# A table of places in a list scheduler's order: every operation named by class, 45 classes moved, three of the scheduler's figures changed

## The chip, the cores and the metric

The kernel runs on one core of a Trainium2 chip. The metric is device time in microseconds. The core has five engines with queues of their own: PE (TensorE, matrix products, with its weight loads shown as PEld), DVE (VectorE), ACT (ScalarE), POOL (GpSimd) and SP (SyncE, which here only issues DMAs). An engine works through its own instructions in the order in which the program gave them and waits at semaphores for the others.

## The reference

Three layers on 2304 tokens of width 512, in fp32:

```python
# attention with random features (4 batches, 8 heads, 576 tokens, head width 64, 128 features)
h = x @ omega.T - sum(x*x)/2;  phi = exp(h - max(h)) / sqrt(128)      # for q and k, both scaled
kv = k_p^T v;  z = sum(k_p);   out = (q_p kv) / (q_p z + 1e-6)
# eight experts, all of them for every token, gates P normalized by 8 Sinkhorn rounds
P = exp(x @ w_gate - max); repeat 8: P /= rowsum; P /= colsum; P *= N/E
out += P[:, e] * (relu(x @ w1[e]) @ w2[e])                            # w1[e] 512x1024, w2[e] 1024x512
# one MLP
g = h * sigmoid(1.702 h),  h = x @ w_in;  out = g @ w_out              # 512x2048 and 2048x512
```

## The kernel before

**Products.** Tokens lie in three blocks of 768 (the "columns" of the program's outer loop, j = 0, 1, 2). The hidden width is worked through in 20 "pairs" of 2 x 256: 16 pairs for the eight experts, two for each, then 4 for the MLP. For each pair and block (a "visit") the products up and down are done with a Strassen scheme of seven products of half-size blocks in place of eight. Each operand is split into a high and a low part that TensorE's fast fp32 form can take, and each product is three matmuls with the terms high-high, high-low and low-high. `up_fast` issues the up products (L1210, 128x384), `down_across` those of the experts' down step (L1364, 128x384), `down` those of the MLP (L1401, 128x256).

**What surrounds them.** After each up product ACT copies banks of PSUM to other banks, to the `ring` in SBUF, or into `h`, the high part of an operand (all L1220, in `act` and `operand`). DVE adds and subtracts banks (L1231), multiplies by the gate (L1252) and makes low parts; low parts from the ring and the sums in the ring are made on POOL or DVE by the helper `tt` (L440). The weights of the next pair are loaded by DMA into `raw`, summed there (L440 on `raw`), and split: ACT makes the high part (L1116, in `split`), POOL the low part (L440 on `w1x`, `w2x`), in three pieces for each of two columns c, one of 128x768 and two of 128x512. After the experts the blocks of x for the MLP are built in the same way by `y_operands` (tiles `acc`, `x2s`; in this stretch POOL does most of it). `double_piece` turns the MLP's weights, which arrive in double precision, into fp32 by six bit steps on DVE (L1140 to L1156) and one sum on POOL, between 440 and 1400 us.

**Attention** runs first, to about 143 us: transposes on PE, copies on ACT, the features' max (L628) and the division (L737, L742, L745) on DVE, exponentials on ACT (L650), squares on POOL. `x_parts` then transposes its results (L785) and splits them (ACT L803, DVE L806) into the operands of the first pairs.

**What sets the order.** The program doesn't issue its instructions as it is written. Each is recorded as an `Op` in a `Plan` with an engine, an estimated duration, and the keys it reads and writes; `VP` means DVE or POOL, `AV` means ACT or DVE. PE's main operations keep their written order. `deadlines` gives each other operation a time `late` at which it must begin so that the main operations that hang on it are not held up: it goes back from each successor's `late` and takes off `LAT` and the operation's duration. `run` then plays all engines through in time. An engine that is free takes, among the operations whose inputs are there, the one with the smallest `late`:

```python
late = min((s.late for s in o.succ), default=total + 50.0) - self.LAT - self.least(o)
...
if e == "DVE" and slack > self.BELOW and len(both) < 14:
    flex = None                       # DVE leaves a VP operation with that much time to POOL
...
at[e] = o.end if e in ("PE", "X") else o.end - self.LEAP
```

`LAT` is the time from an engine to another, `LEAP` how far an engine's next instruction overlaps the last. What `run` returns is the order in which the instructions are written to the engines' queues; the chip's semaphores, not the planned times, decide when they run.

## Time and profile before

| what | us |
|---|---|
| median of 3 runs (1954.36, 1960.79, 1962.69) | 1960.79 |
| the profiled execution's own time | 1957.73 |
| its span in the trace | 1955.8 |
| PE busy | 1925.2 |
| DVE, POOL, ACT busy | 1392.0, 1374.2, 1051.7 |

The profile is of one execution. Busy is the time in which an engine had an instruction at work; it says nothing of whether others waited. Matmuls follow each other closer than one lasts, so TensorE can lose time without a gap in its busy time. The timeline merges like instructions that follow each other into one row with a count. Releasers ("<-") are inferred from semaphores.

### The profile page before, as it was taken

Reading aid. Unit: us, or ns where it says so; the run is one execution under the profiler, and the core shown is the slowest. Engines: PE = TensorE matmul, PEld = TensorE weight load, DVE = VectorE, ACT = ScalarE, POOL = GpSimd, SP = SyncE. Lnnn points to the kernel's source line nnn. Section 1 sums busy time; section 2 is a strip of 40 time slices with the busy share of each in tenths; the row PEclk is TensorE's granted clock in tenths of the full one; section 3 lists DMA queues with packets and bytes.
Section 4 is the critical chain, followed back from the end, with each engine's and each line's share of the span. In section 5 each row is a group of like instructions: output and inputs, shape, how many; then the busy total and the mean of one; then the engine's idle time right before and its main releaser. Section 6 shows DMA issues by size and latency. Waiting matters only on the chain. (4 is left out here: it accounts for less than half of the span.)

```text
span 1955.8 us, 36203 instructions
## 1 busy us (share of the span) xinstructions
PE 1925.2 (98%) x12899; PEld 1883.9 (96%) x12899; DVE 1392.0 (71%) x2704; ACT 1051.7 (54%) x2400; POOL 1374.2 (70%) x1387
## 2 busy tenths in 40 slices
PE   8999999999999999999999999999999989999999
PEld 7888999999999999999999999999999989999999
DVE  6874467767778778778778778778666684656655
ACT  7985554444535445445536345454446476755654
POOL 7965475987759596777769596867758895837452
PEclk9999999999999999999999999999999999999999
DMA  9777556667668576667667576677666788745653
GB/s 175 192 203 245 190 194 244 228 217 279 227 237 293 210 270 257 237 257 267 231 253 272 213 287 243 236 273 254 221 233 252 272 300 316 258 182 201 240 207 125
DMA packets 259292, 464.04 MB, mean 237 GB/s; under 512 B 75288, under 2 KB 200104, under 8 KB 259112
## 3 DMA queue, kind: packets, MB, share of 16 engines
q1 hardware_dynamic: 259112, 461.74, 67.5%
q8 instruction: 101, 1.65, 0.3%
q14 instruction: 79, 0.65, 0.1%
HBM read 415.45 MB, written 46.21 MB: 236 GB/s over the span
## 5 line engine op out<-in xcount | busy, mean ns | idle before, releaser
L1210 PE MATMUL bank<-xo,w1x 128*128 128x384 f32 x5040 | 916.6, 336 | 5.1 <-ACT bank L1220 1.9
L1210 PEld LDWEIGHTS bank<-xo,w1x 128*128 128x128 f32 x5040 | 874.7, 188 | 12.5 <-ACT bank L1220 6.1
L1364 PE MATMUL bank<-h,w2x 128*128 128x384 f32 x4032 | 728.8, 337 | 2.3 <-DVE h L1231 1.3
L1364 PEld LDWEIGHTS bank<-h,w2x 128*128 128x128 f32 x4032 | 700.7, 188 | 8.0 <-POOL h L440 3.4
L440 POOL TENSOR_TENSOR h<-ring,h 128x384 fp32r<-128x384 f32 x452 | 458.2, 1043 | 77.7 <-ACT h L1220 69.3
L1382 DVE TENSOR_TENSOR acc<-bank,acc 128x384 f32<-128x384 f32 x552 | 294.1, 557 | 218.0 <-PE bank L1364 211.0
L440 POOL TENSOR_TENSOR w1x<-raw,w1x 128x768 fp32r<-128x768 f32 (+1 forms) x120 | 179.4, 1504 | 213.1 <-ACT w1x L1116 213.0
L1220 ACT ACTIVATE ring<-bank 128x384 f32<-128x384 f32 x480 | 234.9, 493 | 151.1 <-PE bank L1210 141.6
L1220 ACT ACTIVATE bank<-bank 128x384 f32<-128x384 f32 x216 | 103.6, 482 | 387.7 <-PE bank L1210 358.7
L440 POOL TENSOR_TENSOR raw<-raw 128x256 f32<-128x256 f32 x311 | 242.2, 804 | 75.5 <-DMA raw<-in_moe_w_dram 60.9
L1220 ACT ACTIVATE h<-ring 128x384 fp32r<-128x384 f32 x480 | 237.8, 530 | 77.1 <-DVE ring L1231 71.2
L1231 DVE TENSOR_TENSOR h<-bank,h 128x384 fp32r<-128x384 f32 x324 | 179.0, 553 | 113.4 <-ACT ring L1220 88.9
L440 POOL TENSOR_TENSOR ring<-ring 128x384 f32<-128x384 f32 x114 | 121.2, 1063 | 160.1 <-ACT ring L1220 111.1
L1231 DVE TENSOR_TENSOR ring<-bank,ring 128x384 f32<-128x384 f32 x432 | 223.7, 550 | 9.4 <-ACT bank L1220 6.2
L1252 DVE SCALAR_TENSOR_TENSOR bank<-bank,x2s 128x384 f32<-128x384 f32 x336 | 185.1, 558 | 57.5 <-PE bank L1210 56.8
L1220 ACT ACTIVATE h<-bank 128x384 fp32r<-128x384 f32 x360 | 177.2, 493 | 42.5 <-DVE bank L1252 27.2
L440 POOL TENSOR_TENSOR w2x<-raw,w2x 128x768 fp32r<-128x768 f32 (+1 forms) x120 | 183.9, 1545 | 16.2 <-ACT w2x L1116 15.5
L1401 PE MATMUL bank<-w2x,h 128*128 128x256 f32 x1512 | 186.8, 281 | 5.1 <-POOL w2x L440 2.4
L1401 PEld LDWEIGHTS bank<-w2x,h 128*128 128x128 f32 x1512 | 183.3, 189 | 7.5 <-POOL w2x L440 2.6
L1116 ACT CAST w2x<-raw 128x512 fp32r<-128x512 f32 (+1 forms) x120 | 80.2, 692 | 130.9 <-POOL raw L440 121.6
L1231 DVE TENSOR_TENSOR bank<-bank,ring 128x384 f32<-128x384 f32 x240 | 134.1, 559 | 16.3 <-PE bank L1210 14.6
L1427 DVE TENSOR_TENSOR acc<-bank,acc 128x256 f32<-128x256 f32 x180 | 68.0, 419 | 47.0 <-PE bank L1401 40.9
(134 smaller groups left out, 1263.7 us busy)
## 6 DMA issues: line engine op xcount, KB each, us to landing
xo<-sx SPq DMA_DIRECT2D x413, 768.0 KB, 7.0
raw<-in_moe_w_dram SPq DMA_DIRECT2D x256, 128.0 KB, 4.1
x2s<-scr_g SPq DMA_DIRECT2D x90, 192.0 KB, 6.8
sx<-acc SPq DMA_DIRECT2D x46, 192.0 KB, 2.4
x2s<-in_moe_w_in_dram SPq DMA_DIRECT2D x16, 512.0 KB, 8.2
x2s<-in_moe_w_out_dram SPq DMA_DIRECT2D x16, 512.0 KB, 8.1
sx<-x2s SPq DMA_DIRECT2D x35, 192.0 KB, 4.0
sx<-xo SPq DMA_DIRECT2D x42, 128.0 KB, 2.9
```

Of the source, the lines that this page charges most:

```text
L440: lambda e: e.tensor_tensor(out=out(), in0=a(), in1=b(), op=op), r, w,
L1116: lambda e, a=a, b=b: nc.scalar.copy(T[w, c, 0][:, a:b], r[:, a:b]), raws, [(w, c, g, 0)],
L1210: nc.tensor.matmul(o(b), T["w1", c, a][:, slot, kk], T["xo"][x][:, y, kk], start=start and kk == 0 and n == 0, stop=kk == 1 and n == 2, sk ...
L1220: rec("ACT", act_us(Q), lambda e: nc.scalar.activation(out(), src(), f, **kw), r, w)
L1231: lambda e: e.tensor_tensor(out=out[0](), in0=a[0](), in1=b[0](), op=op), [a[1], b[1]], [out[1]],
L1252: lambda e: e.scalar_tensor_tensor(out=out[0](), in0=o(b), scalar=0.0, in1=T["G"][th], op0=ALU.max, op1=ALU.mult),
L1364: nc.tensor.matmul(bank[i][:, :Q], T["w2", c, y][:, slot, k * P : (k + 1) * P], T["h", c, a, x], start=s and m == 0, stop=c == 1 and m == ...
L1382: lambda e, i=i, q=q: e.tensor_tensor(out=q, in0=bank[i][:, :Q], in1=q, op=ALU.add), rd + [key], [key],
L1401: nc.tensor.matmul(bank[i][:, u], T["h", c, a, x][:, t * P : (t + 1) * P], T["w2", c, y][:, slot], start=s and m == 0, stop=c == 1 and m = ...
L1427: lambda e, q=q, i=i, u=u: e.tensor_tensor(out=q, in0=bank[i][:, u], in1=q, op=ALU.add),
```

## The change

Each operation gets a name, its class (`tag`): the step that it belongs to, with the column where there is one, and a suffix for the stage: `a` in the first pair, `<` in the last pair of the experts, `>` in the first of the MLP, `y` for the MLP's steps. `URGE` gives 45 of these classes a number of microseconds that is added to `late` before the order is made. A negative number moves all operations of the class towards the front of their engine's queue, a positive one towards the back. PE's main operations are left out. Of the scheduler's figures `LAT` goes from 0.17 to 0.072, `BELOW` from 2.5 to 2.608, `LEAP` from 0.07 to 0.087. No operation is added, taken away or altered; those that may run on either of two engines can change engine: seven more run on POOL (1385 for 1378), six fewer on DVE and one fewer on ACT.

```diff
+URGE = {
+    "Dy": 1.2, "d1<": 3.2, "dcy": -0.6, "dec+": 8.4, "dec<": 2.1, "dec>": 1.4, "dy4": -6.6, "gates<": 0.8,
...
+    "r221y": -0.8, "raw": -8.3, "rsum<": 4.0, "s41y": 0.3, "u21<": 0.2, "w1hi1a": 1.6, "w1lo0<": 0.4,
+    "w2hi1<": -0.5, "xhi0": -0.2, "xhi1": 0.8, "xlo0": 2.6, "xo": 7.9, "ymix0<": -7.0, "ymix1<": 1.0,
+}
-    LAT = 0.17
-    BELOW = 2.5
+    LAT = 0.072
+    BELOW = 2.608
     AHEAD = 3.0
-    LEAP = 0.07
+    LEAP = 0.087
     RESTART = 0.1
...
+        self.stage = ""
...
-    def add(self, eng, dur, fn, r=(), w=(), main=False, nb=0.0, lag=0.0, due=None):
+    def add(self, eng, dur, fn, r=(), w=(), main=False, nb=0.0, lag=0.0, due=None, tag=""):
         o = Op()
+        o.tag = tag and tag + self.stage
...
         total = self.deadlines()
+        for o in self.ops:
+            if not o.main:
+                o.late += URGE.get(o.tag, 0.0)
...
-    def tt(out, a, b, op, n, r, w, eng="VP"):
+    def tt(out, a, b, op, n, r, w, eng="VP", tag=""):
...
-            rec("DVE", us, s, R + W, W, due=at + 8.0 + 4.0 * i)
+            rec("DVE", us, s, R + W, W, due=at + 8.0 + 4.0 * i, tag="dec")
```

Three places in the order. The names are those of tiles with a running number that differs between the two programs; lines after the change are higher by 7 to 20.

DVE in attention, before: the denominator (L737), its reciprocal (L742), the max over features of a later tile (L628), the division (L745).

```order
L737 TENSOR_SCALAR acc1_73<-pair_104 128x8
L806 TENSOR_TENSOR xo_76<-bank5_100,xo_76 128x2x2x128
L742 RECIPROCAL acc1_73<-acc1_73 128x8
L628 TENSOR_REDUCE acc1_73<-view0_108 128x2x4
L745 TENSOR_TENSOR acc2_74<-pair_104,acc1_73 128x512
L644 TENSOR_REDUCE acc1_73<-acc1_73 128x8
```

The same place after the change, the division at L759 and the max at L642:

```order
L751 TENSOR_SCALAR acc1_73<-pair_104 128x8
L756 RECIPROCAL acc1_73<-acc1_73 128x8
L759 TENSOR_TENSOR acc2_74<-pair_104,acc1_73 128x512
L617 TENSOR_SCALAR b215_95<-bank4_99 128x512
L642 TENSOR_REDUCE acc1_73<-view0_108 128x2x4
L820 TENSOR_TENSOR xo_76<-bank5_100,xo_76 128x2x2x128
L658 TENSOR_REDUCE acc1_73<-acc1_73 128x8
```

The division has passed the max, the split of x (L820) has gone behind both, and a copy (L617) that was ACT's stands between.

ACT in the first visit of a pair of the experts, before. `h000` is the high part of the first operand in column 0, `bank2<-bank3` the copy of one bank to another in column 1, `w2x` the high parts of the next w2 weights.

```order
L1116 CAST w2x_71<-raw1_68 128x768
L1220 ACTIVATE h000_2335<-bank2_2325 128x384
L1220 ACTIVATE ring_69<-bank2_2325 128x384
L1116 CAST w2x_71<-raw1_68 128x512 x2
L1220 ACTIVATE bank2_2325<-bank3_2326 128x384
L1220 ACTIVATE ring_69<-bank4_99 128x384
L1220 ACTIVATE h060_2347<-bank7_2490 128x384
L1220 ACTIVATE ring_69<-bank7_2490 128x384
L1220 ACTIVATE h010_2337<-bank1_2324 128x384
L1220 ACTIVATE h100_2349<-bank2_2325 128x384
```

After the change:

```order
L1131 CAST w2x_71<-raw1_68 128x768
L1239 ACTIVATE h000_2328<-bank2_2317 128x384
L1239 ACTIVATE ring_69<-bank2_2317 128x384
L1131 CAST w2x_71<-raw1_68 128x512
L1239 ACTIVATE bank2_2317<-bank3_2318 128x384
L1131 CAST w2x_71<-raw1_68 128x512
L1239 ACTIVATE h060_2340<-bank7_2484 128x384
L1239 ACTIVATE ring_69<-bank7_2484 128x384
L1239 ACTIVATE ring_69<-bank4_99 128x384
L1239 ACTIVATE h010_2330<-bank1_2316 128x384
L1239 ACTIVATE h100_2342<-bank2_2317 128x384
```

The copy from bank3 to bank2 has passed one of the two weight copies; the copies of bank7 have passed the one of bank4.

POOL at the switch from the experts to the MLP, before. `w2x` are the low parts of the MLP's first w2 weights, `h...` low parts of operands, `raw` sums of weights; `raw0` belongs to column 0 and `raw1` to column 1.

```order
L440 TENSOR_TENSOR w2x_71<-raw0_67,w2x_71 128x512
L440 TENSOR_TENSOR w2x_71<-raw1_68,w2x_71 128x512
L440 TENSOR_TENSOR h041_2344<-ring_69,h040_2343 128x384
L440 TENSOR_TENSOR raw0_67<-raw0_67 128x256
L440 TENSOR_TENSOR raw1_68<-raw1_68 128x256
L440 TENSOR_TENSOR h141_2358<-ring_69,h140_2357 128x384
L440 TENSOR_TENSOR w2x_71<-raw0_67,w2x_71 128x512
```

After the change, to the same last row:

```order
L454 TENSOR_TENSOR h121_2347<-ring_69,h120_2346 128x384
L454 TENSOR_TENSOR w2x_71<-raw1_68,w2x_71 128x512
L454 TENSOR_TENSOR h041_2337<-ring_69,h040_2336 128x384
L454 TENSOR_TENSOR h141_2351<-ring_69,h140_2350 128x384
L454 TENSOR_TENSOR x2s_75<-x2s_75,acc1_73 128x384
L454 TENSOR_TENSOR h151_2353<-ring_69,h150_2352 128x384
L454 TENSOR_TENSOR acc2_74<-acc2_74,acc1_73 128x384
L454 TENSOR_TENSOR raw0_67<-raw0_67 128x256
L454 TENSOR_TENSOR raw1_68<-raw1_68 128x256
L454 TENSOR_TENSOR x2s_75<-acc2_74 128x384
L454 TENSOR_TENSOR w2x_71<-raw0_67,w2x_71 128x512
```

Between the last piece of 512 for column 1 and the next for column 0 there stood four operations before, and eight now; those that are new come from DVE or from behind.

## Rows read from the trace of the kernel before

**Rows 1.** The page, busy time, share and instructions of each engine.
```profile
PE 1925.2 (98%) x12899; PEld 1883.9 (96%) x12899; DVE 1392.0 (71%) x2704; ACT 1051.7 (54%) x2400; POOL 1374.2 (70%) x1387
```

**Rows 2.** Windows: stretch, length, busy of each engine (count), granted clock, DMA share, GB/s.
```profile
150.00:190.00 40.00, 36.09 (x223) 32.09 (x220) 19.82 (x39) 20.39 (x45) 22.70 (x26) 1.00 0.93 297
320.00:1400.00 1080.00, 1077.56 (x6162) 1068.10 (x6161) 840.59 (x1596) 523.60 (x1111) 802.28 (x758) 1.00 0.69 250
1400.00:1520.00 120.00, 120.00 (x692) 119.84 (x691) 79.95 (x157) 58.55 (x123) 87.06 (x87) 1.00 0.67 239
1560.00:1607.00 47.00, 40.61 (x223) 38.61 (x222) 41.01 (x67) 34.43 (x76) 46.06 (x40) 0.98 0.87 309
1685.00:1956.00 271.00, 265.71 (x1890) 263.91 (x1889) 160.35 (x345) 150.26 (x348) 142.65 (x135) 0.99 0.54 197
```

**Rows 3.** Waits: engine line <- what it waited for: total us, times, longest.
```profile
PE pair L667 <- DVE acc L745: 2.9, 3, 1.1
...
PEld bank L1210 <- ACT bank L1220: 6.1, 12, 1.1
...
PEld bank L1364 <- POOL h L440: 3.4, 19, 0.2
```

**Rows 4.** Timeline, attention: start, duration, engine, line, operation, out<-in, [idle before <-releaser].
```profile
47.84 1.23 DVE L628 TENSOR_REDUCE acc<-view 128x8 f32<-128x1024 f32 x1 [0.18 <-PE view L619]
48.98 0.68 DVE L745 TENSOR_TENSOR acc<-pair,acc 128x512 f32<-128x512 f32 x1
...
49.72 1.15 PE L667 MATMUL pair<-b,acc 128*64 128x65 f32 x32 [0.90 <-DVE acc L745]
```

**Rows 5.** Timeline, 150 to 157, ACT and then PE.
```profile
154.55 0.61 ACT L1116 CAST w2x<-raw 128x512 fp32r<-128x512 f32 x1
155.56 0.37 ACT L803 CAST acc<-bank 128x256 fp32r<-128x256 f32 x1 [0.41 <-PE bank L785]
...
156.45 0.52 PE L828 MATMUL bank<-xo,wg 128*16 128x384 f32 x2 [0.92 <-DVE acc L806]
```

**Rows 6.** Timeline of one expert pair, first and second visit, ACT and PE.
```profile
618.27 1.14 ACT L1116 CAST w2x<-raw 128x512 fp32r<-128x512 f32 x2
619.30 0.49 ACT L1220 ACTIVATE bank<-bank 128x384 f32<-128x384 f32 x1
...
618.22 6.55 PE L1210 MATMUL bank<-xo,w1x 128*128 128x384 f32 x34
...
648.71 5.53 PE L1210 MATMUL bank<-xo,w1x 128*128 128x384 f32 x31
...
651.74 0.49 ACT L1220 ACTIVATE ring<-bank 128x384 f32<-128x384 f32 x1 [0.88 <-PE bank L1210]
```

**Rows 7.** Timeline around the switch, PE.
```profile
1605.38 1.86 PE L1401 MATMUL bank<-w2x,h 128*128 128x256 f32 x7 [2.43 <-POOL w2x L440]
...
1671.48 1.69 PE L1401 MATMUL bank<-w2x,h 128*128 128x256 f32 x12 [0.62 <-DVE h L1231]
```

**Rows 8.** Timeline around the switch, DVE, POOL and PE.
```profile
1566.00 1.37 DVE L440 TENSOR_TENSOR x2s<-acc 128x384 f32<-128x384 f32 x1
...
1583.05 1.01 POOL L440 TENSOR_TENSOR x2s<-x2s 128x384 fp32r<-128x384 f32 x1
...
1594.40 1.33 POOL L440 TENSOR_TENSOR acc<-acc,acc 128x384 fp32r<-128x384 f32 x1
...
1603.34 1.99 POOL L440 TENSOR_TENSOR w2x<-raw,w2x 128x768 fp32r<-128x768 f32 x1
...
1608.23 2.86 POOL L440 TENSOR_TENSOR w2x<-raw,w2x 128x512 fp32r<-128x512 f32 x2
...
1612.35 2.17 POOL L440 TENSOR_TENSOR raw<-raw 128x256 f32<-128x256 f32 x2
...
1615.78 3.18 POOL L440 TENSOR_TENSOR w2x<-raw,w2x 128x512 fp32r<-128x512 f32 x2
...
1613.78 8.49 PE L1401 MATMUL bank<-w2x,h 128*128 128x256 f32 x65
```

176 lines of the change are left out of this document (92 added, 84 removed), and 3 rows, old and new, of the table URGE.

## The prediction

> **What bounds the kernel now.** I read the page's line of busy time first. TensorE is busy 1925.2 of 1955.8 us, and no other engine is above 71% [rows 1]. The windows come next, since they show where TensorE's waits lie [rows 2]. The granted clock in them is 0.98 to 1.00, the upper of the two levels (2.4 GHz), so what can be won is the time in which TensorE waits. From 1400 to 1520 TensorE never waits: 692 matmuls in 120.00 us, 0.1734 us for each. At that rate the 6162 matmuls of 320 to 1400 take 1068.5 us. The stretch lasts 1080, so 11.5 us are lost there, in small pieces that the busy column hides because matmuls overlap. From 150 to 190 TensorE is idle for 3.9 us, from 1560 to 1607 for 6.4 us (with POOL busy 46.06 of 47, the only stretch in which another engine is full), and from 1685 to the end for 5.3 us, most of which is the tail behind the last matmul. Third I read the waits of PE and of its weight loads [rows 3], to learn who ends these pieces, and then timelines at the places which they name. The change adds and removes no instruction. It orders them anew, so its worth is the sum over those places.
>
> **Attention.** PE waits three times, 2.9 us in all, for DVE's division L745 [rows 3]. The reader is to see the first of them [rows 4]: the division begins at 48.98 behind a max over features (L628) that took DVE from 47.84 for 1.23 us. PE starts at 49.72, 0.9 late. In the changed order the division stands ahead of the max at all three places. It takes 0.68 us, so in the place of the max it would end near 48.5, and PE, which had waited 0.90, would have been held for none of it. What is late next is the max itself: by the 0.68 of the division, and in this place by a copy from PSUM as well that came to DVE from ACT (L617 in the new numbering), which I put at the same length. It releases the exponentials on ACT, and PE takes them up only some transposes later. I take the whole 2.9 and round to **-3**; bounds -4 (a few smaller waits for the same operation) and 0 (the delayed max takes the place).
>
> **150 to 180 us.** PE waits 0.92 us at 156.45 [rows 5]. The reader is to follow it back on ACT: a weight copy (L1116) ran from 154.55 to 155.16, then ACT waited 0.41 for a transpose on PE, and the copy that feeds the logits began at 155.56. In the changed order these weight copies stand behind the copies of x, and one transpose goes ahead of a product on PE. With 3.9 us idle in this window as the ceiling, I take half, **-2**; bounds -3 and +0.5.
>
> **The expert pairs.** In the first visit of a pair PE waits for the copy of one bank into another (L1220), which on ACT stands behind two weight copies. Row for row [rows 6]: the two copies take 618.27 to 619.41, the bank copy ends at 619.79, and PE's 34 matmuls last 6.55 us. In the second visit of the pair 31 of them last 5.53; three more at 0.1734 make 6.05. So 0.50 is lost. With 14 pairs from the third to the sixteenth that is 7.0 us. The same wait is 6.1 us in 12 places at the weight loads, and 3.4 us in 19 places are waits for POOL's low halves in the down phase [rows 3]. In the changed order the bank copy stands ahead of the second of the two weight copies, which brings it forward by 0.5 us, about what is lost. The weight copy that it passes is read by POOL only some 5 us later, so the swap costs nothing; without that cover it would cost 0.6 us on POOL in each pair. In the up phase DVE is also rid of most bit steps of the double-precision weights (L1140 to L1156), which go into the down phase between the sums. DVE is busy 840.59 of 1080 there, so there is room. I take **-7**. Bounds: -11.5 (all that is lost in the stretch) and +5 (the second rival's wait, in a fifth of the visits).
>
> **The switch from experts to the last layer (1520 to 1685).** Here POOL is the bound. PE waits 2.43 us up to 1605.38, because the first piece of the new w2 (768 wide, 1.99 us on POOL) ends only at 1605.33 [rows 7, 8]. What is won shortly before 1600 is swallowed there as long as that piece lands when it did. The order puts one more sum of weights on POOL ahead of it, a cost of 1.1 [rows 8], and the 0.94 us in which POOL is idle from 1560 to 1607 [rows 2], with the gaps before 1560, can take that in: I take -0.4 for its landing. The bad part comes behind it. Counted on POOL from the end of that piece to the end of the last 512-wide piece for column 0, it was 12.0 us (1605.33 to 1617.37 [rows 8]). Now there stand one 768-wide piece (1.99), three of 512 (1.43 to 1.59, half of the rows' 2.86 and 3.18), three sums of weights (1.09, half of 2.17) and eight operations of 128x384, which cost 1.01 to 1.33 [rows 8]. Together this is 17.6 to 20.7 us, less 0.5 since neighbours on POOL overlap a little: 17.1 to 20.2. PE first reads the piece with the 42nd of the 65 matmuls in the row that begins at 1613.78, so at about 1618.9, 13.5 us after the first piece. A new wait of 3.6 to 6.7 us follows. I take 4, near the lower end, since the operations came off DVE and POOL will more often be alone. Against it stand 0.62 at 1671.48 (a low half that DVE made late goes to POOL [rows 7]) and some 0.5 of smaller waits that the new one swallows. -0.4 + 4 - 0.6 - 0.5 = **+2.5**; bounds -4 (POOL uses its gaps, the 2.43 goes and no new wait comes) and +5.2 (the wait is 6.7).
>
> The row behind this choice: two POOL operations of one shape, 1.01 and 1.33 us, the longer beside a DVE operation of two SBUF inputs that itself took 1.37 [rows 8]. The Trainium skill, "SBUF — State Buffer", section "Who interferes with whom", says that a DVE instruction with two SBUF inputs contends with a GpSimd instruction that reads SBUF, and that of two that want the shared ports the later one is blocked until the first is done. The row agrees that they contend but not that one is blocked throughout: both got longer by a part. By the rule the work moved from DVE to POOL would cost the pair of engines nothing, the wait would be 3.6, and the sum below 0.4 us better; by the dearer row throughout it would be 6.7, and the sum 2.7 us worse.
>
> **The end (1685 on).** The classes with y in their names move a place here and there; 5.3 us of idle with the tail among them is the ceiling [rows 2]. I count 0, bounds -1.5 and +2.
>
> **Sum.** -3 - 2 - 7 + 2.5 + 0 = -9.5 on the profiled execution's 1957.73 us (span 1955.8 and 1.9 around it): 1948.2. That execution is 3.1 below the median of the runs, 1960.79, and from the median the sum gives 1951.3. The runs spread over 8 us, so I stay close to the profile: **1948**. Its own range is 1942 to 1954.
>
> **Rivals.**
>
> 1. *The switch eats more, the pairs give less.* If POOL runs beside DVE at 1.33 throughout, the switch costs +5.2, and if the freed bank copy then waits for its own source, the pairs give only 3: -3 - 2 - 3 + 5.2 = -2.8, so 1955. For it speaks the full POOL of 1560 to 1607; against it that DVE loses the operations that made POOL slow. Time 1952 to 1958.
>
> 2. *Slower: the copy u21 is late in every visit.* The copy of a bank to the ring for column 1 (L1220, at 651.74 in the second visit of a pair) lets the next product on PE begin. PE's row from 648.71 shows no loss there: 30 starts at 0.1734 make 5.20 of its 5.53 us, and the last matmul's own length is the rest [rows 6]. In the changed order two operand copies stand ahead of u21 on ACT in all visits, and DVE makes a low half before the gate product on which the second of the two waits. On the rows' durations u21 then ends about 0.1 us before PE wants it, 0.2 to 0.3 later than now. If the gate products come later than I think, each of 48 visits loses the length of one ACT copy, 0.49: +23.5, less the 9.5 of the sum: 1957.7 + 14 = 1972. It decides from a slip of 0.2 us on; the +5 among the bounds of the pairs is this in part of the visits.
>
> 3. *More than the sum.* The gaps of POOL are used, and the wait at 1605.38 goes with those before it: switch -4, pairs -10: -3 - 2 - 10 - 4 = -19, so 1939 (1957.7 less 19). For it speaks that POOL's gaps are partly waits for ACT and DVE, whose work also moved; against it the eight operations of 128x384 that now stand between the w2 pieces.
>
> **How the numbers follow.** This kernel's measurement can tell about 0.5%, 9.8 us, from no change: faster is below 1951.0, slower above 1970.6. Forecast 0.53, first rival 0.26, second 0.08, third 0.13. The forecast's range lies below 1951 with three quarters of its chance, 0.40 of 0.53; with the third rival and a little of the first that is 0.54 for faster. Slower is the second rival, 0.08. Same is the rest, 0.38. The range from 1937 to 1959 holds the forecast, nearly all of the first rival and most of the third.
>
> **What would show it.** Right: in attention no wait of PE for the division; from 320 to 1400 fewer than 5 us lost by the count of matmuls, and no weight load that waits for the bank copy; a new wait of PE for a w2 piece of POOL near the switch, some 14 us behind the first. Wrong: waits of PE for an ACT copy into the ring in visit after visit (second rival), the loss of 320 to 1400 unchanged (the swap on ACT did nothing), or a DVE or ACT operation that ends TensorE's idle time where the division did.

## The result and the profile after

The changed kernel is slower: 1973.65 us median of 11 runs (1961.54 to 1983.54) against 1956.45 of 11 runs of the kernel before (1954.36 to 1962.69). The ratio is 1.0095, 95% interval [1.0073, 1.0117], against the forecast of 1948 and outside its range of 1942 to 1954. A second series gave 1980.63 against 1958.37, ratio 1.011 [1.0091, 1.0129]. The profiled execution took 1982.25 us, its span is 1979.7, so it is 24.5 above the profiled execution of before and 8.6 above the median of its own series: the account below is of one of the longest of its runs. Lines after the change are higher by 14 to 19 in the parts read here: L1364 is now L1382 (down products), L1210 L1226 (up products), L1220 L1239 (ACT's copies), L1231 L1250, L1252 L1270, L1382 L1400 (sums of the down phase on DVE, `acc<-bank,acc`), L1116 L1131, L440 L454, and the six bit steps stand at L1156 to L1172.

The page, busy time of each engine, answers [rows 1]:

```profile
PE 1931.6 (98%) x12899; PEld 1890.2 (95%) x12899; DVE 1398.8 (71%) x2698; ACT 1046.9 (53%) x2399; POOL 1365.8 (69%) x1394
```

Three of the windows of [rows 2]:

```profile
150.00:190.00 40.00, 36.12 (x216) 33.87 (x217) 16.89 (x33) 21.59 (x48) 21.41 (x24) 1.00 0.87 279
320.00:1400.00 1080.00, 1060.75 (x6043) 1051.95 (x6043) 829.06 (x1551) 505.69 (x1077) 774.98 (x742) 0.99 0.68 244
1560.00:1607.00 47.00, 45.76 (x258) 44.13 (x256) 33.96 (x60) 26.70 (x58) 44.47 (x44) 1.00 0.85 292
```

The reader is to see the count of matmuls from 320 to 1400: 6043, where there were 6162. At the rate of the prediction, 0.1734 us each, that is 1047.9 us of work in 1080, so 32.1 us are lost, 20.6 more than before. Here PE's busy time has fallen too (1060.75 for 1077.56), so TensorE now has real gaps, where it had small pieces hidden by overlap.

Who ends the gaps, PE's waits and then those of the weight loads (columns as in [rows 3]):

```profile
PE bank L1382 <- DVE acc L1400: 9.9, 2, 9.7
PE bank L1226 <- ACT ring L1239: 7.2, 15, 1.3
PE bank L1420 <- POOL w2x L454: 5.0, 3, 2.1
PE bank L1226 <- ACT bank L1239: 4.5, 1, 4.5
PE bank L1420 <- ACT w2x L1131: 3.7, 2, 3.3
...
PE pair L731 <- DVE acc L759: 1.2, 1, 1.2
...
PEld bank L1226 <- ACT ring L1239: 12.2, 16, 1.7
...
PEld bank L1226 <- ACT bank L1239: 4.9, 1, 4.9
```

The waits of [rows 3] for the division in L667 and for the bank copy in 12 places are gone. In their place stand one wait of 9.7 us for a sum of DVE, one of 4.5 for a copy of ACT, fifteen for the copy into the ring, and five at the switch for pieces of w2.

**The place of the 9.7 us.** Timeline of the changed kernel at 508, DVE (columns as in [rows 4]):

```profile
507.41 1.01 DVE L1400 TENSOR_TENSOR acc<-bank,acc 128x384 f32<-128x384 f32 x2
508.34 11.68 DVE L1163 TENSOR_SCALAR x2s<-x2s 128x512 uint32<-128x512 uint32 x1
519.93 1.94 DVE L1400 TENSOR_TENSOR acc<-bank,acc 128x384 f32<-128x384 f32 x4
```

The same stretch on POOL:

```profile
505.09 6.90 POOL L454 TENSOR_TENSOR h<-ring,h 128x384 fp32r<-128x384 f32 x7
511.95 1.26 POOL L454 TENSOR_TENSOR w1x<-raw,w1x 128x512 fp32r<-128x512 f32 x1
513.17 3.45 POOL L454 TENSOR_TENSOR raw<-raw 128x256 f32<-128x256 f32 x5
516.57 1.80 POOL L454 TENSOR_TENSOR w2x<-raw,w2x 128x768 fp32r<-128x768 f32 x1
518.33 1.40 POOL L454 TENSOR_TENSOR raw<-raw 128x256 f32<-128x256 f32 x2
523.60 1.28 POOL L454 TENSOR_TENSOR w2x<-raw,w2x 128x512 fp32r<-128x512 f32 x1 [3.87 <-ACT w2x L1131]
```

And on PE:

```profile
504.75 6.06 PE L1382 MATMUL bank<-h,w2x 128*128 128x384 f32 x34
520.53 5.79 PE L1382 MATMUL bank<-h,w2x 128*128 128x384 f32 x18 [9.72 <-DVE acc L1400]
```

A bit step of the double-precision weights (L1163), whose median over its 32 places is 0.42 us, lasts 11.68. It begins while POOL is in a row of instructions without a gap; twelve of them begin and end while it lasts, and it ends 0.29 us after the last of them (518.33 + 1.40 = 519.73; 508.34 + 11.68 = 520.02). Behind it on DVE stand the down sums that free PE's banks. I call this a hold. What a hold costs goes on behind it, in the windows of the changed kernel (columns as in [rows 2]; the granted clock is the third figure from the end):

```profile
510.00:520.00 10.00, 0.81 (x5) 0.49 (x3) 10.00 (x2) 0.83 (x1) 9.73 (x12) 0.78 0.49 189
520.00:525.00 5.00, 4.47 (x14) 4.47 (x15) 3.65 (x8) 0.62 (x1) 1.28 (x1) 0.50 0.11 34
525.00:530.00 5.00, 5.00 (x28) 5.00 (x27) 2.24 (x5) 0.50 (x2) 0.00 (x0) 0.92 0.43 131
```

After nearly 10 us of idle TensorE was granted 0.50, the lower level (1.2 GHz): in 520 to 525 it was busy for 4.47 us with 14 matmuls, and in the next 5 us there are 28. A second hold, the first bit step L1156, on DVE, and what PE waits for behind it:

```profile
882.77 9.29 DVE L1156 TENSOR_SCALAR x2s<-x2s 128x512 uint32<-128x512 uint32 x1
...
897.25 2.13 PE L1226 MATMUL bank<-xo,w1x 128*128 128x384 f32 x7 [4.55 <-ACT bank L1239]
```

DVE's sums and low halves behind it come late, then ACT's copy of a bank, then PE.

**Where the 24 us came in.** The start of the same matmul in the two traces (us):

| place | before | after | after less before | step |
|---|---|---|---|---|
| attention, late | 138.0 | 132.0 | -6.0 | -6.0 |
| ahead of the first hold | 423.1 | 417.2 | -6.0 | 0 |
| behind it | 535.9 | 541.9 | +6.0 | +11.9 |
| ahead of the second | 800.3 | 807.8 | +7.6 | +1.6 |
| behind it | 918.0 | 931.6 | +13.6 | +6.0 |
| before the switch | 1507.3 | 1522.9 | +15.6 | +2.0 |
| behind the switch | 1678.0 | 1701.4 | +23.4 | +7.8 |
| the execution's time | 1957.73 | 1982.25 | +24.5 | +1.1 |

The stretches around the two holds are 17.9 of it.

### The profile page after: what moved, and what is told of

Same layout as the page of the kernel before. It is cut to its first block, busy times and chain, and to the rows that moved or that the text cites. A ratio compares the mean times of both kernels' runs of the same rounds, so it can differ in the third digit from the quotient of the medians.

```text
span 1979.7 us, 36262 instructions
## 1 busy us (share of the span) xinstructions
PE 1931.6 (98%) x12899; PEld 1890.2 (95%) x12899; DVE 1398.8 (71%) x2698; ACT 1046.9 (53%) x2399; POOL 1365.8 (69%) x1394
## 4 chain that ended last, share of the span: by engine, by line
PE 82%; DVE 7%; ACT 3%; POOL 3%; DMA 2%; issue 2%; SPq 0%; DVEq 0%; ACTq 0%; POOLq 0%
PE bank L1226 35%; PE bank L1382 31%; PE bank L1420 8%; PE view L633 2%; ACT h L1239 1%; DVE x2s L1163 1%; PE pair L731 1%; PE bank L610 1%; PE pair L681 1%; DVE bank L1270 1%; ACT ring L1239 1%; PE bank L711 1%; DVE h L1250 1%; POOL h L454 1%; DMA sx<-acc 1%
## 5 line engine op out<-in xcount | busy, mean ns | idle before, releaser
L1226 PE MATMUL bank<-xo,w1x 128*128 128x384 f32 x5040 | 919.6, 337 | 12.4 <-ACT ring L1239 7.2
L1226 PEld LDWEIGHTS bank<-xo,w1x 128*128 128x128 f32 x5040 | 876.0, 188 | 20.5 <-ACT ring L1239 12.2
L1382 PE MATMUL bank<-h,w2x 128*128 128x384 f32 x4032 | 731.8, 338 | 12.9 <-DVE acc L1400 9.9
L1382 PEld LDWEIGHTS bank<-h,w2x 128*128 128x128 f32 x4032 | 703.3, 189 | 19.4 <-DVE acc L1400 11.3
L454 POOL TENSOR_TENSOR h<-ring,h 128x384 fp32r<-128x384 f32 x454 | 464.3, 1050 | 94.8 <-ACT h L1239 81.8
L1400 DVE TENSOR_TENSOR acc<-bank,acc 128x384 f32<-128x384 f32 x552 | 292.5, 555 | 196.9 <-PE bank L1382 195.9
L1239 ACT ACTIVATE bank<-bank 128x384 f32<-128x384 f32 x216 | 102.5, 478 | 416.4 <-PE bank L1226 363.4
L1239 ACT ACTIVATE ring<-bank 128x384 f32<-128x384 f32 x480 | 232.7, 491 | 144.9 <-PE bank L1226 126.3
L454 POOL TENSOR_TENSOR w1x<-raw,w1x 128x768 fp32r<-128x768 f32 (+1 forms) x120 | 178.0, 1491 | 184.1 <-ACT w1x L1131 183.7
L454 POOL TENSOR_TENSOR raw<-raw 128x256 f32<-128x256 f32 x313 | 234.9, 776 | 51.3 <-DMA raw<-in_moe_w_dram 38.5
L1239 ACT ACTIVATE h<-ring 128x384 fp32r<-128x384 f32 x480 | 236.3, 528 | 62.2 <-DVE ring L1250 59.0
L1250 DVE TENSOR_TENSOR h<-bank,h 128x384 fp32r<-128x384 f32 x324 | 177.2, 551 | 128.0 <-ACT ring L1239 99.2
L1270 DVE SCALAR_TENSOR_TENSOR bank<-bank,x2s 128x384 f32<-128x384 f32 x336 | 186.0, 558 | 78.4 <-PE bank L1226 75.5
L454 POOL TENSOR_TENSOR ring<-ring 128x384 f32<-128x384 f32 x116 | 119.4, 1029 | 165.7 <-ACT ring L1239 113.5
L1250 DVE TENSOR_TENSOR ring<-bank,ring 128x384 f32<-128x384 f32 x432 | 221.9, 547 | 10.9 <-ACT bank L1239 9.0
L1239 ACT ACTIVATE h<-bank 128x384 fp32r<-128x384 f32 x360 | 175.5, 491 | 69.0 <-DVE bank L1270 54.4
L454 POOL TENSOR_TENSOR w2x<-raw,w2x 128x768 fp32r<-128x768 f32 (+1 forms) x120 | 178.9, 1508 | 27.8 <-ACT w2x L1131 25.8
L1131 ACT CAST w2x<-raw 128x512 fp32r<-128x512 f32 (+1 forms) x120 | 80.5, 692 | 131.6 <-POOL raw L454 100.0
L1250 DVE TENSOR_TENSOR bank<-bank,ring 128x384 f32<-128x384 f32 x240 | 133.3, 558 | 12.0 <-PE bank L1226 9.5
```

What stands on the lines that cost most here:

```text
L454: lambda e: e.tensor_tensor(out=out(), in0=a(), in1=b(), op=op), r, w, tag=tag,
L1131: lambda e, a=a, b=b: nc.scalar.copy(T[w, c, 0][:, a:b], r[:, a:b]), raws, [(w, c, g, 0)],
L1226: nc.tensor.matmul(o(b), T["w1", c, a][:, slot, kk], T["xo"][x][:, y, kk], start=start and kk == 0 and n == 0, stop=kk == 1 and n == 2, sk ...
L1239: rec("ACT", act_us(Q), lambda e: nc.scalar.activation(out(), src(), f, **kw), r, w, tag=tag + z)
L1250: lambda e: e.tensor_tensor(out=out[0](), in0=a[0](), in1=b[0](), op=op), [a[1], b[1]], [out[1]],
L1270: lambda e: e.scalar_tensor_tensor(out=out[0](), in0=o(b), scalar=0.0, in1=T["G"][th], op0=ALU.max, op1=ALU.mult),
```

## The experiments

All compare with the kernel before on the same chip, medians. The letters of theories in the expectations belong to the run in which they stand.

**The order, a piece at a time.** Both orders are made, and the program takes one up to a main operation of PE and the other from there. Only the numbers differ:

```diff
-        for e, o in plan.run():
+        for e, o in plan.mixed([(1, 1125), (0, None)]):   # order_attention: changed up to 1125, then before
+        for e, o in plan.mixed([(0, 1125), (1, 8000), (0, None)]):                 # order_pairs
+        for e, o in plan.mixed([(0, 8000), (1, None)]):                            # order_switch
+    def mixed(self, parts):
...
+        for new, until in parts:
+            for e, o in orders[new]:
+                if o.n == until:
+                    break
+                if o.n not in done:
+                    done.add(o.n)
+                    out.append((e, o))
```

> The order of the changed kernel up to the first up product (143 us in the profile of before), the order of before from there, spliced queue by queue; no figure or table beyond that. By the start times of the same products in the two profiles the attention alone is 6.0 us faster. Theory S (the stages add up): 5 to 7 us faster than before, about 1951, with the same narrow spread. Rival C (the gain is lost again, since the pairs behind are bound by POOL or by DMAs): within 2 us of before.

> The order of before in attention and from 1481 us on (the last pair of the experts and the MLP), that of the changed kernel between. By the profiles this stretch is 3.5 us slower without the two held bit steps and 21.7 with them. Theory H (holds: in this order bit steps stand directly behind a sum into acc, L1400, beside an unbroken chain of POOL, and now and then one is held to the chain's end): 1960 to 1985, spread of the runs over 8 us, and a DVE instruction of over 3 us in the profile. Rival U (the copy u21 and the low parts, not the holds, cost the time): 1958 to 1962, narrow.

> The order of before up to 1481 us, that of the changed kernel from there. By the profiles this stretch is 8 us slower. Theory S: 6 to 10 us slower than before, 1963 to 1968, with PE waiting for pieces of w2 from POOL. Rival D (the switch was slow only because the pairs before it had shifted against the DMAs): within 3 us of before.

Measured against 1955.52: attention 1955.08, ratio 1.0 [0.9991, 1.001]; pairs 1977.57, 1.0112 [1.0098, 1.0125], or +22.0 us; switch 1962.60, 1.0036 [1.0024, 1.0048], or +7.1. The attention alone was expected to win 5 to 7 us and the median shows nothing. The order of the pairs costs 22.0 us and that of the switch a third as much. Not all of the 22.0 is lost in the pairs, so that 21.7 had been expected is in part luck: by the start times in the profile of `order_pairs`, 15.1 us come in between the products of 423 and 1560 us (times of before), 11.0 of them around the hold shown next, and 5.1 more between those of 1560 and 1600, where the order is that of before again and a DVE sum of two SBUF tiles lasts 6.61 us. The spread of over 8 us that was expected didn't come: its four runs lie within 2.0. In order_pairs the same bit step is held for as long as in the changed kernel (its lines are higher by 18):

```profile
512.31 11.68 DVE L1181 TENSOR_SCALAR x2s<-x2s 128x512 uint32<-128x512 uint32 x1
```

Attention alone wins 5.4 us by 138 us and gives 5.0 of them back by 154.5 (2.7 come again by 180 in this profile), where PE now waits for the low half of x on which the gate's products hang (DVE L838, which is L806 of before):

```profile
PE bank L860 <- DVE acc L838: 5.0, 2, 4.1
```

**The table without the figures, the figures without the table.** `figs_only` takes the kernel before with `LAT`, `BELOW`, `LEAP` of the change, `urge_only` the changed one with the old three.

```diff
# figs_only, against before       # urge_only, against after
-    LAT = 0.17                    -    LAT = 0.072
+    LAT = 0.072                   +    LAT = 0.17
-    BELOW = 2.5                   -    BELOW = 2.608
+    BELOW = 2.608                 +    BELOW = 2.5
-    LEAP = 0.07                   -    LEAP = 0.087
+    LEAP = 0.087                  +    LEAP = 0.07
```

> The three figures of the change without the table. In this order the division stands ahead of the max (attention should gain 5 to 6 us), and the bit steps stand in the down phase behind d1 and d3, where POOL works without gaps. Theory P: holds of 5 to 12 us come in some runs, which spread over more than 8 us; median 1955 to 1972. Rival T: the table was the harm, so without it the gain stays: 1946 to 1952, within 4 us of each other.

> The table of the change with the scheduler's three figures as before. In this order the division in attention stands behind the max as before, and the bit steps stand in the up phase as before. Theory P: no holds, since what moved the bit steps into the down phase is the figures; the gain of attention (6 us) is gone too. The rest of the table (pairs, switch) decides: 1955 to 1964. Rival T (the table itself makes the kernel slow, by the switch and the copy u21): 1962 or more, with PE waits for u21 in the first visits.

Measured against 1960.11: figures alone 1986.91, 1.0155 [1.0135, 1.0176]; table alone 1962.76, 1.0024 [1.0014, 1.0034]. So the three figures by themselves lose more than the whole change does, and the 45 classes by themselves 2.7 us. In the traces the figures alone put the division ahead of the max and 94 of the 192 bit steps directly behind a down sum (97 in the changed kernel); the table alone leaves both nearly as they were (51, and 53 before). Which of the three figures does it was not tested. In `urge_only` no bit step is held, but a DVE sum at the switch lasts 5.65 us. In `figs_only` other DVE instructions are held than in the changed kernel, both with two inputs in SBUF:

```profile
373.88 7.00 DVE L440 TENSOR_TENSOR acc<-acc,x2s 128x384 f32<-128x384 f32 x1
...
1595.79 11.18 DVE L440 TENSOR_TENSOR acc<-acc,acc 128x384 fp32r<-128x384 f32 x1
```

These two are not all that the figures alone cost. Between the products of 386 and 1399 us PE loses another 16.0 us in small pieces, though no DVE instruction of that stretch lasts over 2.5 us. The weight loads of the down phase wait for DVE's sums (8.4 us of it in one wait) and for POOL's low halves, the latter for 12.7 us in 22 places where it was 3.4 in 19 [rows 3]:

```profile
PEld bank L1364 <- DVE acc L1382: 13.3, 18, 8.4
PEld bank L1364 <- POOL h L440: 12.7, 22, 0.8
```

So the loss of `figs_only` is in large part another than that of the changed kernel, where all but 3.7 us of the pairs' loss lies around the holds.

**Is it the form of the instruction?** Three of the six bit steps are `tensor_scalar`. Here they are `scalar_tensor_tensor` in the same places, in both kernels (the second step, which has this form already, is altered to fit).

```diff
...
-            lambda e: e.tensor_scalar(
-                out=m(), in0=wh(), scalar1=0x7FFFFFFF, scalar2=None, op0=ALU.bitwise_and
+            lambda e: e.scalar_tensor_tensor(
+                out=m(), in0=wh(), scalar=0x7FFFFFFF, in1=wh(), op0=ALU.bitwise_and, op1=ALU.bitwise_and
...
```

> The changed kernel, with the three bit steps that are tensor_scalar instructions (L1156, L1163, L1169: 0.42 us for 128x512, against 0.68 for a scalar_tensor_tensor of the same size) rewritten as scalar_tensor_tensor with the same results; order and all else as in the changed kernel. Theory P (port): the 9.3 and 11.7 us that two of these steps took lasted exactly as long as POOL worked without a gap, because in their fast form they need what POOL holds. Then no DVE instruction lasts over 3 us, the runs lie within 8 us of each other, and the median is 1960 to 1966 (the profiled 1982.3 less 9.9, 4.7 and some 2.5 of half clock). Rival O (other source): the step waits for something that has nothing to do with its form, such as the DMA that fills its tile; then holds of some 10 us stay in the profile or in the spread of the runs and the median stays at 1970 to 1980.

> The kernel before with the same three steps rewritten as scalar_tensor_tensor. Theory P: the runs of before at 1961 to 1963 are short holds of this kind too, so the spread falls below 4 us and the median is 1952 to 1957; a step that lasted up to 1.52 us beside POOL gets shorter. Rival O: no difference beyond 0.3%, spread as before (8 us). If the 0.26 us more for each step on DVE reaches PE, 1957 to 1962.

Measured against 1960.11: after so altered 1984.94, 1.0133 [1.011, 1.0155]; before so altered 1968.68, 1.0055 [1.0039, 1.0072]. Both lie above all that was expected. The theory that only the single-input form is held fell: the rewritten step is held too.

```profile
876.16 9.60 DVE L1156 SCALAR_TENSOR_TENSOR x2s<-x2s 128x512 uint32<-128x512 uint32 x1
```

The order of before isn't free of holds either. With the longer steps, `one_port_before` has one at the switch, as `order_pairs` has in its part with the order of before:

```profile
1590.72 6.61 DVE L440 TENSOR_TENSOR x2s<-acc 128x384 f32<-128x384 f32 x1
```

**Is it the neighbour?** All holds of a bit step seen by then began right behind a down sum. `spacer` puts a memset of two elements ahead of every bit step.

```diff
...
+            def spaced(e, s=s):
+                nc.vector.memset(tiny, 0.0)
+                return s(e)
-            rec("DVE", us, s, R + W, W, due=at + 8.0 + 4.0 * i, tag="dec")
+            rec("DVE", us, spaced, R + W, W, due=at + 8.0 + 4.0 * i, tag="dec")
```

> The changed kernel, with a memset of two elements per partition on DVE ahead of each of the 192 bit steps, on a tile that nothing reads. Order and all else as in the changed kernel. In six profiles all 13 DVE instructions that let POOL pass more than once stood directly behind a sum acc<-bank,acc (13 of 237 such), none behind another instruction (0 of some 425). Theory B (what stands directly before on DVE decides): no held bit step is left, the runs within 8 us, 1961 to 1968. Rival F (the phase or POOL's chain decides, not the neighbour): holds as before, median 1970 to 1985, an instruction of over 5 us in the profile or a spread of over 10 us.

Measured: 1970.68 against 1955.52, 1.0076 [1.0064, 1.0088]. The hold at 508 is gone, the other is there with the memset right ahead of it, so the neighbour is not the cause:

```profile
871.17 0.06 DVE L1179 MEMSET tiny<- 128x2 f32 x1
871.26 9.14 DVE L1157 TENSOR_SCALAR x2s<-x2s 128x512 uint32<-128x512 uint32 x1
```

**Is it the down phase?** `steps_in_up_phase` moves every bit step that stands behind a down sum behind the next DVE instruction that is none, by passing the order through one more function.

```diff
...
+            if o.n in block or (o.tag == "dec" and (last[:2] in sums or any(x.tag == "dec" for _, x in held))):
+                held.append((e, o))
+                block |= {s.n for s in o.succ}
+                continue
...
```

> The order of the changed kernel, but each bit step that stands directly behind a sum of the down phase (130 of 192) goes behind the next DVE instruction of the up phase. If the holds of DVE in the down phase cost the time (theory H): no bit step over 3 us, 1961 to 1966, spread under 8 us. If the steps are held wherever POOL works without a gap (rival W): holds as before, 1970 to 1985. If the steps now delay the up phase itself, PE waits for DVE there, 1966 to 1975 without a long instruction.

Measured: 2072.32 against 1957.47, 1.0583 [1.0567, 1.0599], the worst run of all and far above all that was expected. The steps are held in the up phase too (5.34 us at 825 and at 927), and there even a step of normal length is in the way of what PE waits for:

```profile
PE bank L1279 <- ACT ring L1292: 42.6, 33, 3.4
PE bank L1279 <- DVE bank L1303: 26.2, 13, 4.2
```

**POOL and DVE by themselves.** POOL runs ten sums of 128x384 back to back, DVE alternates a sum with PSUM and an instruction on SBUF, in 72 cases; in `beside_dma` 144 cases with the start shifted and DMAs writing to SBUF.

```diff
...
+            for i in range(10):
+                G.tensor_tensor(out=cs[i], in0=a, in1=b, op=ALU.subtract)
+            for i in range(4):
+                first(i)     # acc<-bank,acc or bank<-bank,acc
+                second(i)    # tensor_scalar, scalar_tensor_tensor or tensor_tensor, SBUF only
```

> No part of the computation: 72 groups in which POOL makes ten tensor_tensor of 128x384 from SBUF without a gap, while DVE does four times one instruction with a PSUM operand and one without. The first writes to SBUF (a sum into acc) or to PSUM; the second is a tensor_scalar of 128x512 in SBUF, a scalar_tensor_tensor of two SBUF operands, or a tensor_tensor of two. DVE starts in each group at another moment, by a first instruction of growing length. Theory H (POOL and DVE by themselves do this): some of the second instructions last to the end of POOL's ten, 3 to 10 us, and most 0.4 to 1.6. Theory B (the neighbour decides): those behind sums into SBUF only. Rival E (PE's matmuls of the down phase or the DMAs have a part in it): none lasts over 2 us.

> The kernel with POOL and DVE alone once more, 144 cases in place of 72, starts shifted in steps of some 20 ns over 0.5 us, and DMAs that write to SBUF all the while. It computes none of the reference. Theory D (writes of DMAs, or a start at the right phase, let POOL pass DVE): some of the 576 DVE instructions with SBUF operands last over 2.5 us. Theory E2 (something else of the kernel is needed: TensorE's reads, ACT, or the semaphores): none above 1.3 us, as in the first kernel of this kind.

Measured: no hold in either; the longest DVE instruction took 1.27 us in the first and 1.55 in the second. Groups of `beside` (busy, mean ns of one):

```profile
L62 POOL TENSOR_TENSOR pc<-pa,pb 128x384 f32<-128x384 f32 x720 | 778.8, 1116 | 0.0
...
L43 DVE TENSOR_SCALAR dy<-dx 128x512 uint32<-128x512 uint32 x96 | 70.5, 735 | 0.0
```

The two engines lengthen each other (the step of 0.42 us takes 0.735, POOL's sum 1.116 where it takes 0.99 alone), but POOL doesn't pass DVE; 1.55 is a little over the 1.3 that was expected for that case. What more a hold needs is something that these two kernels don't have; they ran without TensorE and ACT.

**Place or chance?** The changed kernel unaltered, twice, and with the two held steps moved behind the next DVE instruction, 2 places of some 2500.

```diff
-        for e, o in plan.run():
+        for e, o in plan.later(plan.run(), (2601, 2707)):
...
```

> The changed kernel once more, unaltered. Its eleven runs lie between 1961.5 and 1983.5, a spread of 22 us where most other kernels here spread over 4 to 9. Theory F (the place of a hold is fixed by the program): its profile has the same two DVE bit steps held as in the first one, 11.7 us at 508 and 9.3 us at 883. Theory V (a hold comes or stays away by chance in each execution, since it hangs on some tens of nanoseconds between the engines): the profile has other steps held, more or fewer, and the times fall into groups: about 1962 with none, 1972 with one long hold, 1982 with two.

> The changed kernel a third time, for one more profile. F: holds at 508 and 883 of 11.7 and 9.3 us, about 1982. V: its time follows the number of long holds in this profile, 1962 and some 10 to 12 us for each.

> The changed kernel with the two bit steps that were held in its profile each moved behind the next DVE operation (a sum of the down phase in both cases), 2 of some 2500 places on DVE. If the two holds are what the change costs (12 and 6 us in the comparison of start times) and belong to these places: 1973.7 - 18 = 1956 to 1964, and no spread of 22 us. If another step is held in their stead: 1970 to 1983 as before, with a hold of more than 5 us elsewhere.

Measured against 1958.37: 1980.63, 1.011 [1.0091, 1.0129]; 1980.49 in a single run; the moved steps 1974.75, 1.0077 [1.0054, 1.01]. Holds of `same_again`, whose profiled execution took 1989.10:

```profile
510.40 11.64 DVE L1163 TENSOR_SCALAR x2s<-x2s 128x512 uint32<-128x512 uint32 x1
...
789.77 8.48 DVE L1156 TENSOR_SCALAR x2s<-x2s 128x512 uint32<-128x512 uint32 x1
...
893.10 9.30 DVE L1156 TENSOR_SCALAR x2s<-x2s 128x512 uint32<-128x512 uint32 x1
```

Of `same_third` (1980.49):

```profile
508.62 11.64 DVE L1163 TENSOR_SCALAR x2s<-x2s 128x512 uint32<-128x512 uint32 x1
...
882.57 9.33 DVE L1156 TENSOR_SCALAR x2s<-x2s 128x512 uint32<-128x512 uint32 x1
```

Of `two_steps_later` (1977.37; lines higher by 18):

```profile
778.73 8.49 DVE L1174 TENSOR_SCALAR x2s<-x2s 128x512 uint32<-128x512 uint32 x1
...
884.14 6.71 DVE L1174 TENSOR_SCALAR x2s<-x2s 128x512 uint32<-128x512 uint32 x1
```

Both theories hold in part. The steps at 508 and 883 are held in all three profiles of the program, so the place matters; one more is held in one of three, so chance does too. Moving the two took away the first hold and shortened the second, a third came, and the time fell to 1974.75 and not to the 1956 to 1964 that were expected.

**Are the holds the cost?** Profiles in which one of the two holds is missing tell it most directly, since their steps keep their length. The start of the same products, less that of before, changes by this much around the two places:

| profile | first hold | 423 to 536 us | second hold | 800 to 918 us |
|---|---|---|---|---|
| the changed kernel | 11.68 | +11.9 | 9.29 | +6.0 |
| `spacer` | none | +0.7 | 9.14 | +6.0 |
| `order_pairs` | 11.68 | +11.0 | none | -0.2 |

Where the hold is missing, so is the loss. In a further test every bit step is cut from 512 columns to 2, in both kernels, in the same places of their orders. This takes away the steps' ordinary length as well as the holds, so it can't tell the two apart by itself.

```diff
...
-        a, m = (lambda: w(0).bitcast(U32)), (lambda: w(1).bitcast(U32))
-        af, mf = (lambda: w(0)), (lambda: w(1))
-        wl, wh = (lambda: r()[:, :, 0]), (lambda: r()[:, :, 1])
+        a, m = (lambda: w(0)[:, 0:2].bitcast(U32)), (lambda: w(1)[:, 0:2].bitcast(U32))
+        af, mf = (lambda: w(0)[:, 0:2]), (lambda: w(1)[:, 0:2])
+        wl, wh = (lambda: r()[:, 0:2, 0]), (lambda: r()[:, 0:2, 1])
...
```

> The changed kernel, with every bit step on DVE cut from 512 columns to 2 in the same place of the same order (the weights of the MLP are then not converted). Theory H (what the change costs in the pairs, some 18 of 22 us, is the steps that are held for a chain of POOL operations): a step of 2 columns reads SBUF so briefly that it is hardly held, so this kernel stands above short_steps_before by the rest alone, -3 (attention) + 4 (copies of the pairs) + 7 (switch) = 5 to 10 us, and its spread is below 10 us. Rival R (the pairs lose by the order on ACT and DVE as such): the difference stays at 18 to 22 us.

> The kernel before with the same cut, as the base for short_steps_after. H and R alike: 1950 to 1957, since DVE waits for nobody in these steps and none of them is held in the kernel before.

Measured: after so altered 1962.42 (1955.34 to 1972.02), before so altered 1953.93 (1952.27 to 1959.55), so 8.5 us between them; 5 to 10 was expected if the holds are the cost in the pairs, 18 to 22 if it is the order as such. Between the unaltered kernels there were 17.2 and 22.3. The expected spread of less than 10 us didn't come: it is 16.7, and no profile shows what the longest of these runs lose. The profiled execution of `short_steps_after` (1956.70) is among the shortest. In it the stretch of the pairs has its matmuls again, here in its windows:

```profile
320.00:1400.00 1080.00, 1079.03 (x6185) 1073.03 (x6184) 759.13 (x1590) 520.19 (x1108) 779.75 (x764) 1.00 0.70 251
```

The wait for the copy into the ring is less than half of the changed kernel's:

```profile
PE bank L1227 <- ACT ring L1240: 3.1, 7, 1.3
```

The timeline shows that even a step of 2 columns is lengthened, but none above this one:

```profile
499.14 1.84 DVE L1161 SCALAR_TENSOR_TENSOR x2s<-x2s 128x2 uint32<-128x2 uint32 x1
```

The profiles stand in one row by their holds of a bit step over 8 us: none, 1956.70 (`short_steps_after`); one, 1969.53 (`spacer`); two, 1982.25 and 1980.49 (the changed kernel); three, 1989.10. Two others fit less plainly: `two_steps_later`, with holds of 8.49 and 6.71, took 1977.37, and `one_port_after`, with one of 9.60 and all its steps longer, 1979.13.

**A version that is faster.** `order_two_pairs` takes the changed order up to main operation 2001 (some 320 us) and that of before from there. `order_bank_copy` has, besides, the swap of the prediction in ten pairs: the copy of the bank passes the last weight copy on ACT.

```diff
+        for e, o in plan.mixed([(1, 2001), (0, None)]):              # order_two_pairs
+        for e, o in plan.swap(plan.mixed([(1, 2001), (0, None)])):   # order_bank_copy
+    def swap(self, out):
...
+            if a.tag == "w2hi1" and b.tag == "pc1":
+                hold[a.n] = b.n
```

> The order of the changed kernel through attention and the first pair (up to some 325 us), the order of before from there. With the cut at the first product the gain of 5.4 us was given back within 10 us behind it (+4.4 at the products of 153 us); the changed kernel itself kept it there. Theory K (the weight copies and the transposes of the first pair have to go with attention): 5 to 6 us faster than before, 1949 to 1951, narrow. Rival C (the pairs behind take it back): within 2 us of before.

> As order_two_pairs, and in ten pairs of the experts the bank copy pc1 passes the one weight copy that stands directly ahead of it on ACT; nothing else of the table. In the profile of before this wait of PE costs 0.2 to 0.9 us, 4.3 us in eleven pairs, with 1.2 of slower starts behind. Theory: 3 to 5 us faster than order_two_pairs, 1945 to 1947. Rival (u21, which stands some places behind on ACT, is late in its place as in the changed kernel): within 1.5 us of order_two_pairs.

Measured against 1957.47: 1952.73, 0.9972 [0.9959, 0.9984], and 1954.18, 0.9983 [0.9973, 0.9993]. The first is faster than both kernels, by 4.7 us or a quarter of a per cent than the one before, a little less than the 5 to 6 expected. The swap was expected to win 3 to 5 us more and adds nothing: from 320 to 1481 us the same products start 0.5 us later than without it, in the two profiles. With the swap the waits for the bank copy are gone, and this has come:

```profile
PE bank L1268 <- ACT ring L1281: 3.6, 12, 0.9
```

In `order_two_pairs` 4.35 us are still lost ahead of the gate's products. DVE's low half of x waits for a DMA that still reads its tile:

```profile
153.98 0.42 DVE L838 TENSOR_TENSOR acc<-bank,acc 128x256 fp32r<-128x256 f32 x1 [4.53 <-DMA sx<-acc]
```

## Why the prediction was wrong

**Attention (-3), 150 to 180 (-2).** -6.0 was measured by 138 us, beyond the bound of -4, and nothing more by 423. The mechanism was right, the step was too small: besides the three waits in L667 smaller ones went, as the lead of 1.1 to 1.4 us at four places in the start times shows. In the place of [rows 4] PE runs without a wait:

```profile
47.09 1.15 PE L681 MATMUL pair<-b,acc 128*64 128x65 f32 x32
```

The 2 us behind it didn't come: at the gate's products PE waits 1.51 for DVE's low half. Together -5 was forecast and -6 measured, which is luck, since one term was half of what came and the other came to nothing. The gain isn't firm: with the order of before behind it, 5.0 of it were lost by 154.5, and the median kept none.

**The pairs (-7): the step that failed.** It cost the bit steps in the down phase at nothing, "DVE is busy 840.59 of 1080 there, so there is room". The busy share says how much time DVE has, not how long an instruction lasts when POOL runs beside it. I had the row for that on the table and used it at the switch alone: two-input work on DVE and POOL lengthen each other [rows 8]. In the down phase DVE's next instruction is the sum that frees PE's bank, and a step that is held stands in front of it. Measured: +21.6 us from 417 to 1523, of which 17.9 around the two holds and 3.7 elsewhere. That the two holds are the cost is shown by the profiles in which one of them is missing (+0.7 and -0.2 in place of +11.9 and +6.0), and the short steps agree (8.5 us left of 17 to 22). The 3.7 are read from two profiles and their places were not tested.

The second half of the step failed as well. The bank copy did come forward and its waits went, as forecast, but the copy into the ring (u21) is the next thing late: fifteen waits, 7.2 us, a part of them because DVE is behind (with short steps 3.1 in seven). `order_bank_copy` shows the swap without the bit steps: 3.6 us of the new wait, no gain. So the -7 wasn't there to be had by this swap. Without the steps' length the changed order is faster than that of before by 1.8 us from 423 to 1481, in the profiles of the two kernels with short steps; that is what is left of the -7.

The Trainium skill, "SBUF — State Buffer", "Who interferes with whom", has it that of a DVE and a GpSimd instruction that want the shared ports the second to issue is blocked until the first is done. By that rule a bit step would wait for one POOL instruction, 0.99 us here (6.90 for seven), and a hold as in the changed kernel couldn't last over twelve. The measurement decides: usually DVE gets longer by a part, and rarely it is passed by the whole row. In the changed kernel a `tensor_scalar` bit step takes 0.42 us where POOL is idle and 0.73 (median of 35) where POOL works all the while. Of the DVE instructions of 128x384 or 128x512 without a PSUM operand that began inside a POOL instruction with at least two more close behind it, 2 of 96 were passed by two or more whole POOL instructions in the changed kernel, 2 of 110 in `order_pairs`, 0 of 133 in the kernel before. Before has more such meetings and none is held in its one profile, so some fine point of timing seems to decide. Which, is open: the first step was held when it began 0.28 to 0.31 us into a POOL instruction in the changed kernel's three profiles and in `order_pairs`, the second at 0.62 in the three, other steps at other moments, and shifting the start in `beside_dma` found no hold.

**The switch (+2.5).** +7.8 by the start times, +7.1 alone in `order_switch`: the right sign, beyond the upper bound of +5.2. The rows of PE at the switch, in the changed kernel:

```profile
1620.87 0.38 PE L1420 MATMUL bank<-w2x,h 128*128 128x256 f32 x1 [3.34 <-ACT w2x L1131]
1623.13 2.07 PE L1420 MATMUL bank<-w2x,h 128*128 128x256 f32 x8 [1.87 <-POOL w2x L454]
...
1632.25 6.51 PE L1420 MATMUL bank<-w2x,h 128*128 128x256 f32 x53 [1.02 <-POOL w2x L454]
1639.12 0.38 PE L1420 MATMUL bank<-w2x,h 128*128 128x256 f32 x1 [0.36 <-ACT w2x L1131]
1641.65 4.86 PE L1420 MATMUL bank<-w2x,h 128*128 128x256 f32 x26 [2.15 <-POOL w2x L454]
```

The new wait for a late piece is there: it ends at 1641.65, 18.5 us behind the first piece (1623.13), and 17.1 to 20.2 had been worked out for the landing. It is smaller (2.15 and 0.36) than the 3.6 to 6.7, since PE itself came to the piece later than the 13.5 us that were taken from before. What the sum left out is ACT: the high part (L1131) of the first piece came late too, 3.34 us. For pieces of w2 PE waits 8.7 us in all, 5.0 and 3.7, and waited 2.43 for POOL before [rows 7] and 1.4 for ACT. From 1620 to 1630 the granted clock was 0.66 on average. The row behind the choice of +4 was misread as well: the DVE operation of 1.37 us at 1566.00 had ended long before POOL's 1.33 at 1594.40 began [rows 8], so the two are no pair. In the same trace POOL has two operations from 1564.32 that take 2.64 together beside DVE's at 1564.71 and 1566.00, 1.37 each, so the reading that both get longer stands.

**The end (0).** +1.1, within its bounds.

**The rivals.** The slower one, 1972 for u21 in every visit, lies nearest to the time, but by another mechanism: u21 waits in 15 visits, not 48, and isn't the main cost. The first rival's dearer switch (+5.2) came, and more, but not its gain in the pairs. No rival named a DVE instruction that POOL holds, though the prediction weighed the rule for it.

## What to carry to other kernels

An instruction moved to a place where its engine "has room" must be costed by what stands right behind it and by what the engine with which it shares ports does at that moment; the busy share of the stretch says neither. When a wait is cleared by bringing one copy forward, look for the next copy in the same queue that the same engine waits for, and try the swap alone: here the second took back the whole gain. A reordering is best taken apart by stretches: the changed order up to some 320 us and the old one behind it is faster than both (0.9972), though the whole is 1% slower. Look at the profile of each piece too: `order_pairs` lost 5.1 of its 22.0 us where its order was the old one.

## What the runs showed that was not expected

- A DVE instruction of 0.42 us can last 5 to 11.7 us while POOL runs instruction after instruction; seen in both forms of the bit steps and in sums of two SBUF tiles, in the down phase, the up phase and at the switch, never on an instruction with an operand in PSUM.
- A hold ends with POOL's row. In all 32 DVE instructions of over 2.5 us in the profiles of this kernel and its variants, POOL's row breaks for at least 0.49 us, and the DVE instruction ends 0.28 us (`tensor_scalar`), 0.41 (`tensor_tensor`) or 0.55 (`scalar_tensor_tensor`) after the row's last instruction. So what a hold costs is the rest of the row.
- It recurs at the same place of the same program (508 and 883 in three of three profiles), and comes at another in one of the three (790). The changed kernel's runs spread over 27.6 us (1961.54 to 1989.10 in 18 runs), those of before over 7 to 10 in each series.
- A wait of 9.7 us of TensorE was followed by a granted clock of 0.50 in the next 5 us; the same products came 11.9 us later behind it.
